# One step of a recurrent attention rebuilt: where the precomputed projections, the softmax waits and the output projection of the tail run

## The chip, the cores and the metric

The kernel runs on one core of one Trainium2 chip. The metric is the device time of one execution in microseconds. Three runs of the kernel before took 2381.08, 2387.85 and 2399.44 us, so the median is 2387.85 us. One execution was profiled; its own time is 2384.49 us and its span, from the first to the last instruction, 2382.6 us.

## The reference, cut to what matters

```python
# A: x [2048, 1024] in 64 segments of 32 rows; mem [8, 1024]; H = 32 heads of 128
mem = mem0
for s in range(64):
    h = concat([mem, x[32*s : 32*s+32]])          # 40 rows
    q, k, v = h @ Wq, h @ Wk, h @ Wv               # each 1024 -> 32 x 128
    p = softmax(mask(q @ k.T * 128**-0.5))         # per head, 40 x 40
    o = (p @ v) @ Wo                               # 4096 -> 1024
    mem = o[:8]                                    # goes into the next segment
    outs.append(o[8:])
a = concat(outs)
# B: a GEGLU feed-forward on x, 1024 -> 3584 -> 1024
b = (gelu(x @ w_gate) * (x @ w_up)) @ w_down
g = sigmoid(sum(x * gate_w))
return g * a + (1 - g) * b
```

The 64 segments are a chain: the memory rows of one are needed before the first projection of the next.

## The kernel before, in words

**Stages.** A first stage transposes x into scratch in DRAM and loads weights. Then come 64 steps, one for each segment, then a tail that multiplies the remaining attention rows by Wo, then the feed-forward.

**Rows.** A step projects 32 columns: the 24 first rows of its segment and the 8 memory rows (`hT`). The other 8 rows of each segment depend on no memory, so their q, k and v are computed for four segments at once, from the 32 columns in `hR`, by *fill units* (`fill`, L690): 8 pieces of 4 matmuls. A fill unit's result is copied out of PSUM, for q and k also transposed, put in one of the `stage` buffers and written to `qk_scr` or `v_scr` by DMAs that POOL issues; later steps read it back into `qkr` and `vB`. `FILL` (L738) says which of the six units of a group runs in which of four steps: two units, two, one and one. The attention output of these 8 rows is collected in `oRc`, written to `o_scr`, and multiplied by Wo in the tail (L867 to L886): 256 matmuls of 512 columns.

**Weights.** Wq, Wk, Wv and Wo are cut into 64 *pieces* of 512 KB ([128, 2048]). 53 slots of SBUF hold them. 42 pieces stay; 22 pieces form 11 pairs, the two of a pair sharing one slot (`PAIRS`, L304). Each step uses both halves r = 0 and r = 1 of every matrix and swaps their order from step to step (`at_step`), so each pair costs one fetch a step (`fetch`, `spent`): SP issues it as soon as the piece in the slot has been used, and it has to have landed when the other half of the same matrix comes to it.

**Order in a step.** `ORDER` (L310) gives 8 blocks of 8 pieces: k0 (positions p0 to p7), q0 (p8 to p15), v0 (p16 to p23), k1 (p24 to p31), q1 (p32 to p39), o0 (p40 to p47), v1 (p48 to p55), o1 (p56 to p63). A piece of k, q or v is 4 matmuls of 512 columns, on four column groups of the array at a time; a piece of o is 8 of 256 columns. `on(m, r, n, ...)` hooks other work in front of piece n of a block, in the program order of every engine: ACT copies a finished block to `tok` or `vA` (L570), PE transposes `tok` (L587), DVE copies that to `kT` or `qT` (L573), `scores` (L603) runs 33 small matmuls and the softmax on DVE and ACT into `tA` and `tB`, and `attend` (L634) multiplies those by `vA` and `vB` into four banks, from where ACT and DVE copy to `oT`, which the o block reads.

The first softmax is started before k1 and its attend stands in q1 at its sixth piece; the second is started before v1 and its attend stands before o1, with 6 pieces of a fill unit around v1 in the steps that have two units, 3 in the others. At the end of a step ACT copies the o result to `a_bf`, PE transposes it (L845) and DVE writes the 8 memory columns into `hT` (L848); other fill pieces stand around that transpose.

**Shared memory.** The tiles of the step share their bytes: `vA` lies on `oT`, and so does the stage buffer "o"; stage "k" lies on `kT` together with `pA` and `pB`; stage "q" on `qT` together with `tA`, `tB`, `E8` and `a_bf`. A tile is written only when every reader of the bytes is done, DMAs included: `vA` waits until the store of stage "o" has landed.

**Queues.** Each engine works in program order. SP issues the fetches. POOL issues the small DMAs of the step in one line with its own copies: after the end of a step it stores `a_bf`, then the fill results, then copies `qkr` into `kT` and `qT` (L732), then loads `qkr` and `vB`. These DMAs use a scratch of `RING` bytes in each partition (L253).

## Time and profile before

| | |
|---|---|
| median of three runs | 2387.85 us |
| profiled execution: its time, its span | 2384.49 us, 2382.6 us |
| PE busy | 2071.2 us, 87% of the span |
| DVE, ACT, POOL busy | 898.5 us (38%), 571.7 us (24%), 588.2 us (25%) |
| bytes moved by DMA | 542.61 MB, mean 228 GB/s |
| mean granted clock of TensorE | 0.984 |

The span falls into four stretches: up to 134.6 us the first stage and step 0; up to 1718.3 us the steps 1 to 63; up to 1778.8 us the tail with Wo; then the feed-forward, to the end. The three cuts are the end of step 0 and of step 63 (the copy to `a_bf`) and the first matmul of the feed-forward. Busy shares are averages over all of that; what matters for a change inside the step is what PE waits for inside a step. The time outside the span is 1.9 us.

### The profile page before, as it was taken

To read this page: it belongs to the slowest core of one execution; us is meant where nothing else is said; L and a number is where in the kernel's file an instruction comes from. 1 tells how busy PE (TensorE), PEld (TensorE's weight loads), DVE (VectorE), ACT (ScalarE), POOL (GpSimd) and SP (SyncE) were. 2 spreads that over 40 slices of the span, in tenths; PEclk is the share of its full clock that TensorE was granted. 3 is DMA by queue.
4 is the path that set the end of the run, shared out by engine and by line. 5 is a ranking of instruction groups with operands and counts; after the bars stand their busy time and mean duration, and the time that the engine had idled before them with its cause. 6 is when DMAs were issued, how large, how long until landed. Compare 5 with 4: busy or idle time off the path is not lost.

```text
span 2382.6 us, 76316 instructions
## 1 busy us (share of the span) xinstructions
PE 2071.2 (87%) x34822; PEld 1059.3 (44%) x34822; DVE 898.5 (38%) x2119; ACT 571.7 (24%) x1175; POOL 588.2 (25%) x1139
## 2 busy tenths in 40 slices
PE   2588888888888888898888988887799999999998
PEld 1244444444444444444444444444464444444443
DVE  3233333333333433334333333333215345263462
ACT  1122222222222222222222222222113123031230
POOL 5233323333233333333333333332200000000000
PEclk9899999999999999999999999998999999999999
DMA  9967776777767767778687776776872440804406
GB/s 355 371 224 243 267 262 235 267 260 265 269 227 253 280 221 285 255 245 290 229 289 246 256 262 239 274 263 212 278 245 109 155 146 1 291 9 145 156 1 229
DMA packets 207970, 542.61 MB, mean 228 GB/s; under 512 B 27288, under 2 KB 40472, under 8 KB 207648
## 3 DMA queue, kind: packets, MB, share of 16 engines
q1 hardware_dynamic: 174240, 483.99, 57.1%
...
q14 instruction: 49, 0.40, 0.0%
...
## 4 chain that ended last, share of the span: by engine, by line
PE 48%; DMA 25%; DVE 12%; issue 6%; ACT 5%; POOL 3%; ACTq 0%; SPq 0%; POOLq 0%
PE pb L918 14%; PE pb L683 10%; PE pb L955 6%; DMA vB<-v_scr 6%; DMA v_scr<-oS 5%; DMA qk_scr<-oS 5%; PE pb L671 5%; PE pb L698 4%; DMA sl<-in_A_Wq_dram 3%; PE pb L877 2%; DMA a_scr<-a_bf 2%; DMA wd<-in_B_w_down_dram 2%; DVE st L620 2%; PE pb L587 2%; POOL v_scr L709 2%
## 5 line engine op out<-in xcount | busy, mean ns | idle before, releaser
L671 PE MATMUL pb<-sl,hT 128*32 128x512 bf16 x12288 | 780.5, 384 | 52.5 <-DMA sl<-in_A_Wk_dram 21.3
L671 PEld LDWEIGHTS pb<-sl,hT 128*32 128x32 bf16 x12288 | 316.6, 96 | 350.8 <-DMA sl<-in_A_Wk_dram 38.6
L683 PE MATMUL pb<-sl,oT 128*32 128x256 bf16 x8192 | 277.4, 282 | 2.6 <-ACT oT L570 2.1
L570 ACT ACTIVATE tok<-pb 128x512 bf16<-128x512 f32 x320 | 191.3, 598 | 319.0 <-PE pb L671 265.3
L683 PEld LDWEIGHTS pb<-sl,oT 128*32 128x32 bf16 x8192 | 211.1, 100 | 60.4 <-ACT oT L570 24.8
L698 PE MATMUL pb<-sl,hR 128*32 128x512 bf16 x3072 | 226.5, 391 | 7.1 <-issue 6.0
L918 PE MATMUL pb<-xT,wg 128*128 128x512 bf16 x896 | 211.8, 379 | 8.4 <-DVE GT L934 8.4
L655 POOL COPY oRc<-oT 128x128 bf16<-128x128 bf16 x128 | 97.2, 759 | 466.5 <-DVE oT L573 466.5
L918 PE MATMUL pb<-xT,wu 128*128 128x512 bf16 x896 | 211.7, 379 | 0.0
L955 PE MATMUL pb<-wd,GT 128*128 128x512 bf16 x896 | 195.9, 379 | 3.4 <-DMA wd<-in_B_w_down_dram 3.3
L641 PE MATMUL pb<-tA,vA 32*128 32x40 bf16 x2048 | 36.5, 178 | 138.4 <-DVE tB L631 94.5
L570 ACT ACTIVATE vA<-pb 128x512 bf16<-128x512 f32 x128 | 76.4, 597 | 289.8 <-DMA v_scr<-oS 126.5
L926 ACT ACTIVATE s<-pb 128x512 f32<-128x512 f32 x112 | 66.8, 596 | 319.8 <-PE pb L918 300.3
L918 PEld LDWEIGHTS pb<-xT,wg 128*128 128x128 bf16 x896 | 86.9, 98 | 116.3 <-DVE GT L934 12.8
L573 DVE COPY kT<-pb 128x512 bf16<-128x512 bf16 x128 | 54.3, 424 | 217.8 <-POOL kT L732 121.2
L955 PEld LDWEIGHTS pb<-wd,GT 128*128 128x128 bf16 x896 | 86.7, 98 | 111.9 <-DMA wd<-in_B_w_down_dram 9.5
L918 PEld LDWEIGHTS pb<-xT,wu 128*128 128x128 bf16 x896 | 87.7, 98 | 105.7
L616 DVE TENSOR_REDUCE st<-pb 128x8 f32<-128x320 f32 x128 | 62.9, 491 | 169.3 <-PE pb L611 169.3
L573 DVE COPY qT<-pb 128x512 bf16<-128x512 bf16 x128 | 54.3, 424 | 192.0 <-PE pb L587 182.5
L927 DVE SCALAR_TENSOR_TENSOR tp<-s,pb 128x512 f32<-128x512 f32 x112 | 76.9, 686 | 131.7 <-ACT s L926 131.6
L570 ACT ACTIVATE oT<-pb 128x160 bf16<-128x160 f32 x256 | 63.8, 301 | 215.0 <-PE pb L646 215.0
L641 PEld LDWEIGHTS pb<-tA,vA 32*128 32x128 bf16 x2048 | 25.0, 92 | 199.0 <-DVE tB L631 97.3
...
## 6 DMA issues: line engine op xcount, KB each, us to landing
sl<-in_A_Wv_dram SPq DMA_DIRECT2D x268, 512.0 KB, 10.4
sl<-in_A_Wk_dram SPq DMA_DIRECT2D x205, 512.0 KB, 6.0
sl<-in_A_Wq_dram SPq DMA_DIRECT2D x142, 512.0 KB, 9.1
sl<-in_A_Wo_dram SPq DMA_DIRECT2D x142, 512.0 KB, 6.0
wd<-in_B_w_down_dram SPq DMA_DIRECT2D x56, 1024.0 KB, 6.5
qkr<-qk_scr POOLq DMA_DIRECT2D x128, 64.0 KB, 5.8
...
```

The lines of the kernel that those rows point to most:

```text
L570: op("act", lambda e: e.activation(o, i, ACTF.Copy), rd=rd, wr=wr)
L573: op("dve", lambda e: e.tensor_copy(o, i), rd=rd, wr=wr)
L616: op("dve", lambda e: e.tensor_reduce(nm, sS, AX.X, ALU.max, negate=True), rd=[BK(SS)], wr=[st8.r(0, 8)])
L641: e.matmul(PB[bo[g]][:, j * LQ:(j + 1) * LQ], lhsT=vA[r, j, :], rhs=tA[r, 2 * j:2 * j + 2, :].rearrange("p a c -> p (a c)")[:, 0:LQ], star ...
L655: op("pool", lambda e: e.tensor_copy(oRc[:, :, 16 * u:16 * u + 16].rearrange("p c x -> p x c"), oT[:, :, :, 32:40].rearrange("p g j c -> p ...
L671: ins = e.matmul(PB[bk][32 * g:32 * g + 32, :], lhsT=h[:, i, :], rhs=w[:, g * 512:(g + 1) * 512], start=(p % 8 == 0), stop=(p % 8 == 7))
L683: ins = e.matmul(PB[XO][32 * g:32 * g + 32, 0:256], lhsT=oT[:, gp_, 2 * jj + hh, 0:32], rhs=w[:, c:c + 256], start=(r == 0 and p % 8 == 0 ...
L698: ins = e.matmul(PB[b][32 * g:32 * g + 32, :], lhsT=h[:, k[2], :], rhs=w[:, g * 512:(g + 1) * 512], start=(n == 0), stop=(n == 7))
L918: ins = e.matmul(PB[bk][:, 0:FB], lhsT=w[:, kc, cc:cc + 128], rhs=xT[:, :, :, kc, :].rearrange("p t i c -> p (t i) c"), start=(kc == 0), s ...
L926: op("act", lambda e, hg=hg: e.activation(s1[:, :], hg, ACTF.Square, scale=SQ), rd=[BK(bg)], wr=[s1.r()])
L927: op("dve", lambda e, hg=hg, t=t: e.scalar_tensor_tensor(out=t[:, :], in0=s1[:, :], scalar=1.0, in1=hg, op0=ALU.add, op1=ALU.mult), rd=[BK ...
L955: ins = e.matmul(PB[bank[2 * k + hf]][:, :], lhsT=GT[:, j, tb * 128:(tb + 1) * 128], rhs=w[:, jj, hf * 512:(hf + 1) * 512], start=(j == 0) ...
```

## The change

**The fill units and where they run.** Every step now has up to two units, one in front of o0 (`f1`, bank F1) and one in front of o1 (`f2`, bank F2). The first attend stands inside f1 (4 pieces, attend, 1 piece, the transpose of q1, 3 pieces), the second inside f2 (5 pieces, attend, 3 pieces). f2 is a q or v unit in each of four steps. f1 is a k unit in two of four steps; in the other two it is a *Wo unit* (`wo`): 8 pieces with the shape of the o pieces, that multiply the collected rows of four earlier segments by one half of Wo. Their two halves are added (`part`, `add_part`) and stored by POOL (`store_tail`). The tail stage is gone but for the last four segments: `last_tail` runs after seven of the 28 blocks of the feed-forward's first part, and the loads w3, w4 and of w_down come behind it.

**The end of a step.** No fill pieces stand around the memory transpose any more. The copy to `a_bf`, the transpose and the copy into the next `hT` are cut in halves, for the even and the odd pieces of k; k0 uses the even pieces first. There are two `hT`, so the next segment's load is issued during q1.

**Buffers.** The two stage buffers, `pA` and `pB` have bytes of their own; `a_bf` lies on `pA`. `qkr` exists twice, and the scores read the q part from it, so that one POOL copy (`rest_k`) remains of two; it stands before the end of the step.

**Weights.** 12 pairs in 52 slots, so 12 fetches a step: k 2 (were 3), q 2, v 5 (were 4), o 3 (were 2). **Ring.** `RING` goes from 4096 to 2048 bytes. The rest of the memory freed holds `oR`, `part` and `oR2`.

**Step 0** computes one fill unit more (q0 of group 1), and its three units for r = 1 stand in front of the first scores instead of behind the first attend.

The diff, cut; lines that the region of the step loses are those of the functions printed above.

```diff
-        RING = 4096
+        RING = 2048
...
-        hT = al("hT", [128, KC, 32])
+        hTs = [al(f"hT{n}", [128, KC, 32]) for n in range(2)]
         hR = al("hR", [128, KC, 32])
         low = cur[0] = (cur[0] + 63) // 64 * 64
-        qkr = al("qkr", [128, 2, 128])
-        oRc = al("oRc", [128, NB, 32])
+        qkr = al("qkr", [128, 2, 2, 128])
+        oRc = al("oRc", [128, 2, NB, 16])
         vB = al("vB", [128, 2, 128])
         kT = al("kT", [128, 4, 4, LQ])
-        qT = al("qT", [128, 4, 4, LQ])
+        qT = al("qT", [128, 4, 4, 32])
         oT = al("oT", [128, 4, 4, LQ])
         tok = al("tok", [128, 512])
+        stage = [al(f"stg{n}", [128, 512]) for n in range(2)]
+        pA = al("pA", [128, 8, 32])
+        pB = al("pB", [128, 288])
+        a_bf = al("a_bf", [128, 256], at=pA.off)
         vA = al("vA", [128, 4, 128], at=oT.off)
-        pA = al("pA", [128, 8, 32], at=kT.off)
-        pB = al("pB", [128, 288], at=kT.off + 512)
-        E8 = al("E8", [128, 8, LQ], at=qT.off + 640)
         tA = al("tA", [128, 8, 32], at=qT.off)
         tB = al("tB", [128, 8, 32], at=qT.off + 512)
-        a_bf = al("a_bf", [128, 256], at=qT.off)
-        stage = {n: al(n + "S", [128, 512], at=t.off) for n, t in (("k", kT), ("q", qT), ("o", oT))}
+        E8 = al("E8", [128, 8, LQ], at=qT.off + 384)
 
         PIECE = 4096
         cur[0] = (cur[0] + 63) // 64 * 64
         res0 = cur[0]
         NLOW = (hole - RING) // PIECE
+        odd0 = RING + NLOW * PIECE
+        assert hole - odd0 >= 2048
+        oR = al("oR", [128, RB, 16], at=odd0)
+        part = al("part", [128, 256], FP32, at=odd0 + 1024)
+        oR2 = al("oR2", [128, RB, 16], at=odd0 + 1024)
         NSLOT = NLOW + (top - cur[0]) // PIECE
 
 
-        PAIRS = {"k": (1, 3, 5), "q": (0, 2), "v": (0, 2, 4, 6), "o": (0, 2)}
+        PAIRS = {"k": (0, 2), "q": (0, 2), "v": (0, 1, 2, 4, 6), "o": (0, 2, 4)}
 
         def seq(m, r):
             p = [i for i in range(8) if i in PAIRS[m]]
...
         def load_h(s):
-            op("pool", lambda e: e.dma_start(hT[:, :, :].rearrange("p k c -> p (k c)"), xq_scr[s // 4, :, s % 4, :]),
-               rd=[("D", "xq", s // 4)], wr=[hT.r()], lane="h")
+            t = hTs[s % 2]
+            op("pool", lambda e: e.dma_start(t[:, :, :].rearrange("p k c -> p (k c)"), xq_scr[s // 4, :, s % 4, :]),
+               rd=[("D", "xq", s // 4)], wr=[t.r()], lane=f"h{s % 2}")
 
...
+        def scores(r, mid=None):
...
-                            ins = e.matmul(PB[SS][32 * g:32 * g + hi - lo, j * 80 + c:j * 80 + c + LQ], lhsT=qT[:, j, g, lo:hi],
-                                           rhs=kT[:, j, g, :], start=False, stop=True, skip_group_check=True)
+                            x = 8 * (4 * j + g)
+                            ins = e.matmul(PB[SS][32 * g:32 * g + hi - lo, j * 80 + c:j * 80 + c + LQ],
+                                           lhsT=qT[:, j, g, :] if lo == 0 else qkr[:, r, 0, x:x + 8], rhs=kT[:, j, g, :], start=False, stop=True, skip_group_check=True)
                 return ins
-            op("pe", f, rd=[qT.r(), kT.r(), ident.r(), mS.r()], wr=[BK(SS)])
...
+        bank_of = {("k", 0): B0, ("q", 0): B1, ("v", 0): B2, ("k", 1): B0, ("q", 1): F2, ("v", 1): B0}
...
-                op("pe", f, rd=[h.r(), w.r()], wr=[BK(bk)])
+                op("pe", f, rd=[h.r(32 * i, 32 * i + 32), w.r()], wr=[BK(bk)])
...
+        def wo(u, b, t=oR, ends=(True, True), at_end=False):
+            out = []
+            for i in range(8):
+                w = (xo.get(("o", u, i)) if at_end else None) or slots[home["o", u, i]]
+
+                def f(e, i=i, w=w):
+                    for hh in range(2):
+                        for g in range(4):
+                            c = hh * 1024 + g * 256
+                            ins = e.matmul(PB[b][32 * g:32 * g + 32, 0:256], lhsT=t[:, :, 2 * i + hh], rhs=w[:, c:c + 256],
+                                           start=(ends[0] and i == 0 and hh == 0), stop=(ends[1] and i == 7 and hh == 1))
+                    return ins
+                out.append(lambda f=f, w=w: op("pe", f, rd=[t.r(), w.r()], wr=[BK(b)]))
+            return out
+
+        def store_tail(Q, t):
+            for g in range(4):
+                op("pool", lambda e, g=g: e.dma_start(a_scr[4 * Q:4 * Q + 4, NR:SEG, 256 * g:256 * g + 256],
+                                                      t[32 * g:32 * g + 32, 0:256]),
+                   rd=[t.r(0, 256)] + [("D", "a", x) for x in range(4 * Q, 4 * Q + 4)], wr=[("D", "ar", Q, g)], lane=f"ar{g}")
...
+        def rest_k(r):
+            op("pool", lambda e: e.tensor_copy(kT[:, :, :, 32:40].rearrange("p j g c -> p (j g) c"),
+                                               qkr[:, r, 1, :].rearrange("p (x c) -> p x c", c=8)),
+               rd=[qkr.r(256 * r + 128, 256 * r + 256)], wr=[kT.r()])
...
-        FILL = ((("k", 1), ("q", 1)), (("q", 0), ("v", 0)), (("v", 1),), (("k", 0),))
-        X, Y = A0, A1
+        FILL1 = {3: ("k", 0), 0: ("k", 1)}
+        FILL2 = {3: ("q", 0), 0: ("q", 1), 1: ("v", 0), 2: ("v", 1)}
         for s in range(NSEG):
             last = s == NSEG - 1
             at = {}
             ua, ub = s % 2, 1 - s % 2
+            h_next = hTs[1 - s % 2]
             G = (s + 1) // 4 + 1
-            fl = [(m, u, G) for m, u in FILL[s % 4]] if G < NG else []
-            bank_of.update({mr: (X, Y)[n % 2] for n, mr in enumerate(KQV)})
-            bko = dict(bank_of)
-            fill_bank = (X, Y)
-            f1 = fill(*fl[0][:2], X) if fl else []
-            f2 = fill(*fl[1][:2], Y) if len(fl) > 1 else []
+            Q = s // 4 - 1
+            k1 = FILL1.get(s % 4) if G < NG else None
+            k2 = FILL2[s % 4] if G < NG else None
+            uw = {1: 1, 2: 0}.get(s % 4) if Q >= 0 else None
+            f1 = fill(*k1, F1) if k1 else wo(uw, F1) if uw is not None else []
+            f2 = fill(*k2, F2) if k2 else []
 
             def on(m, r, n, *fs):
                 at.setdefault(base_of[m, r] + n, []).extend(fs)
                     f()
                 del fs[:n]
 
...
+            on("k", 0, 4, some(pend))
...
+            on("k", 1, 0, lambda: scores(0))
+            on("k", 1, 3, lambda: rest_k(1))
+            on("q", 1, 0, lambda: evac(bank_of["k", 1], tok))
+            if not last:
+                on("q", 1, 0, lambda: load_h(s + 1))
+                on("q", 1, 1, lambda: load_qk(s + 1, 0))
+                on("v", 1, 2, lambda: load_qk(s + 1, 1))
+            on("q", 1, 4, lambda: trans(kT))
+            if s % 4 == 0 and Q >= 0:
+                on("q", 1, 2, lambda: load_oR(Q, 1))
+            if s % 4 == 1 and Q >= 0:
+                on("o", 0, 3, lambda: load_oR(Q, 0))
+            def add_part():
+                op("dve", lambda e: e.tensor_tensor(out=stage[0][:, 0:256], in0=PB[F1][:, 0:256], in1=part[:, :], op=ALU.add),
+                   rd=[BK(F1), part.r()], wr=[stage[0].r(0, 256)])
+            on("o", 0, 0, lambda: evac(bank_of["q", 1], tok))
+            on("o", 0, 0, some(f1, 4))
+            on("o", 0, 0, lambda: attend(ua))
+            on("o", 0, 0, some(f1, 1))
+            on("o", 0, 0, lambda: trans(qT))
+            on("o", 0, 0, some(f1))
+            if k1:
+                on("o", 0, 1, lambda: fill_evac(*k1, F1, stage[0]))
+            if uw == 1:
+                on("o", 0, 1, lambda: act_copy(part[:, :], PB[F1][:, 0:256], [BK(F1)], [part.r()]))
+            on("o", 0, 1, lambda: scores(1, add_part if uw == 0 else None))
+            if k1:
+                on("o", 0, 6, fill_trans)
+                on("o", 0, 6, lambda: fill_put(stage[0], "act"))
+                on("o", 0, 6, lambda: fill_store(*k1, G, stage[0]))
+            if uw == 0:
+                on("o", 0, 6, lambda: store_tail(Q, stage[0]))
+            on("o", 1, 0, lambda: evac(bank_of["v", 1], vA))
+            if not last:
+                on("o", 1, 0, lambda: rest_k(0))
+            on("o", 1, 0, some(f2, 5))
             on("o", 1, 0, lambda: attend(ub))
+            on("o", 1, 0, some(f2))
+            if k2:
+                on("o", 1, 1, lambda: fill_evac(*k2, F2, stage[1]))
             def o_store(s=s):
+                op("pool", lambda e: e.dma_start(o_scr[s].rearrange("p u c -> p (u c)"), oRc[:, :, :, :].rearrange("p u c x -> p (u c x)")),
+                   rd=[oRc.r()], wr=[("D", "o", s)], lane="sto")
+            on("o", 1, 2, o_store)
             if last:
                 for n, f in enumerate(early):
                     on("o", 1, 1 + n, f)
             for p in range(64):
                 run(at.get(p, []))
                 proj(p, s)
+            for t in range(2):
+                cs = slice(128 * t, 128 * t + 128)
+                act_copy(a_bf[:, cs], PB[XO][:, cs], [BK(XO)], [a_bf.r(cs.start, cs.stop)])
+            if k2 and k2[0] == "q":
+                fill_trans()
             if not last:
+                for t, bk in enumerate((B1, B2)):
+                    op("pe", lambda e, t=t, bk=bk: e.transpose(PBV[bk][:, 0:128], a_bf[:, 128 * t:128 * t + 128], ident[:, :]),
+                       rd=[a_bf.r(128 * t, 128 * t + 128), ident.r()], wr=[BK(bk)])
+                    op("dve", lambda e, t=t, bk=bk: e.tensor_copy(
+                        h_next[:, :, NR:32].rearrange("p (g t) c -> p t g c", t=2)[:, t],
+                        PBV[bk][:, 0:128].rearrange("p (g c) -> p g c", g=4)[:, :, NR:32]),
+                       rd=[BK(bk)], wr=[h_next.r(32 * kc, 32 * kc + 32) for kc in range(t, KC, 2)])
+            if k2 and k2[0] == "q":
+                fill_put(stage[1], "dve")
+            def store(s=s, k2=k2, G=G):
                 op("pool", lambda e: e.dma_start(a_scr[s].rearrange("r (g c) -> g r c", g=4), a_bf[:, :]), rd=[a_bf.r()],
                    wr=[("D", "a", s)], lane="st")
+                if k2:
+                    fill_store(*k2, G, stage[1])
             pend.append(store)
             f()
+        load_oR(NG - 1, 1, oR2)
+        load_oR(NG - 1, 0)
+        def last_tail():
+            for f in wo(1, XO, oR2, (True, False), True) + wo(0, XO, oR, (False, True), True):
+                f()
+            t = oR2
+            a_last = al("a_last", [128, 256], at=t.off)
+            act_copy(a_last[:, :], PB[XO][:, 0:256], [BK(XO)], [a_last.r()])
+            store_tail(NG - 1, a_last)
+            load_w(3)
+            load_w(4)
+            for n in range(3):
+                load_wd()
         C_GELU = 0.7978845608028654
         SQ = 0.044715 ** 0.5
...
             for j in range(NJ):
+                if fb == 0 and j == sum(CH[:2]):
+                    last_tail()
```

## Rows read from the trace of the kernel before

**Rows 1.** Stretches of the span: start:end, length, busy by engine, clock, DMA share, GB/s.

```profile
134.60:1718.30 1583.70, 1368.38 (x31020) 728.40 (x31012) 581.45 (x1633) 409.93 (x907) 533.94 (x1073) 0.98 0.73 257
1718.30:1778.80 60.50, 56.73 (x256) 36.93 (x257) 2.07 (x3) 2.77 (x5) 0.73 (x1) 0.97 0.76 245
```

**Rows 2.** PE's groups in the steps: busy, mean ns, then idle and its releasers.

```profile
L671 PE MATMUL pb<-sl,hT 128*32 128x512 bf16 x12096 | 765.2, 382 | 52.5 <-DMA sl<-in_A_Wk_dram 21.3 <-ACT vA L570 18.7 <-issue 4.5
...
L641 PE MATMUL pb<-tA,vA 32*128 32x40 bf16 x2016 | 35.9, 178 | 133.9 <-DVE tB L631 94.5 <-DMA vB<-v_scr 38.9
```

**Rows 3.** ACT's groups in the steps: the copy of v out of PSUM.

```profile
L570 ACT ACTIVATE vA<-pb 128x512 bf16<-128x512 f32 x126 | 75.2, 597 | 279.6 <-DMA v_scr<-oS 120.2 <-DMA qk_scr<-oS 96.7 <-PE pb L671 62.7
```

**Rows 4.** PE in order of time, one step: start, length, operation, idle before.

```profile
1064.53 0.29 PE L845 MATMUL pb<-ident,a_bf 128*128 128x128 bf16 x2
1064.75 1.05 PE L698 MATMUL pb<-sl,hR 128*32 128x512 bf16 x16
1065.62 2.98 PE L671 MATMUL pb<-sl,hT 128*32 128x512 bf16 x52
...
1074.65 1.75 PE L671 MATMUL pb<-sl,hT 128*32 128x512 bf16 x24 [0.69 <-DMA sl<-in_A_Wk_dram]
1077.49 0.27 PE L641 MATMUL pb<-tA,vA 32*128 32x40 bf16 x16 [1.10 <-DVE tB L631]
...
1082.47 0.31 PE L611 MATMUL pb<-kT,qT 128*32 128x40 bf16 x21 [0.85 <-issue]
...
1084.33 0.82 PE L698 MATMUL pb<-sl,hR 128*32 128x512 bf16 x12
1086.53 0.28 PE L641 MATMUL pb<-tA,vA 32*128 32x40 bf16 x16 [1.38 <-DVE tB L631]
...
1086.77 0.61 PE L698 MATMUL pb<-sl,hR 128*32 128x512 bf16 x8
1087.27 1.93 PE L683 MATMUL pb<-sl,oT 128*32 128x256 bf16 x64
1089.02 0.60 PE L698 MATMUL pb<-sl,hR 128*32 128x512 bf16 x8
1089.69 0.29 PE L845 MATMUL pb<-ident,a_bf 128*128 128x128 bf16 x2
```

**Rows 5.** All engines in order of time: one softmax from scores to tB.

```profile
1030.30 0.31 PE L606 MATMUL pb<-mS,ident 128*128 128x320 bf16 x1
...
1034.15 0.40 DVE L631 STREAM_TRANSPOSE tB<-pB 128x256 bf16<-128x256 bf16 x1
```

**Rows 6.** PE in order of time: the end of a step without fill units.

```profile
1667.46 0.29 PE L845 MATMUL pb<-ident,a_bf 128*128 128x128 bf16 x2 [0.48 <-ACT a_bf L570]
1668.03 2.99 PE L671 MATMUL pb<-sl,hT 128*32 128x512 bf16 x52 [0.28 <-DVE hT L848]
```

**Rows 7.** One step's fetches (line L360): issues, first and last start; time to landing.

```profile
L360 SPq DMA_DIRECT2D sl<-in_A_Wv_dram x4: 328/468/803, 1017.6 to 1019.4; - x4
L360 SPq DMA_DIRECT2D sl<-in_A_Wk_dram x3: 328/341/435, 1013.1 to 1014.1; - x3
...
DMA to landing us min/median/max: 4.1/8.0/11.3
```

**Rows 8.** A stretch in which fetches alone run: columns as in Rows 1.

```profile
1023.00:1028.00 5.00, 3.90 (x72) 1.78 (x68) 2.91 (x9) 1.46 (x5) 1.33 (x3) 0.73 1.04 406
```

**Rows 9.** DMA issues by line: count, KB each, median us to landing.

```profile
xT<-xq_scr SPq DMA_DIRECT2D x4, 1024.0 KB, 6.3
...
vB<-v_scr POOLq DMA_DIRECT2D x63, 64.0 KB, 6.3
v_scr<-oS POOLq DMA_DIRECT2D x124, 32.0 KB, 5.6
...
wg<-in_B_w_gate_dram SPq DMA_DIRECT2D x1, 512.0 KB, 8.7
```

**Rows 10.** POOL in order of time, the start of a step.

```profile
1091.24 2.18 POOL L709 DMA_DIRECT2D v_scr<-oS  x4 [0.59 <-ACT oS L570]
```

More of the change, by code (lines that the diff above doesn't have):

```diff
@@ L514, in al2 @@
             raise AssertionError(name)
-        asb = [al2(f"asb{t}", [128, D]) for t in range(4)]
         tp = [al2(f"tp{t}", [128, FB], FP32) for t in range(2)]
         s1 = al2("s1", [128, FB], FP32)
+        assert s1.off < res0
+        asb = [al2(f"asb{t}", [128, D]) for t in range(4)]
         dsb = [al2(f"dsb{t}", [128, 512], FP32) for t in range(2)]
@@ L812, in bass_gated_mix__memory_aug_recurrent_mem_tr__geglu_ffn__prompt_kernel @@
-            on("q", 1, 6, lambda: trans(kT, "dve"))
-            on("q", 1, 7, rest_1)
-            on("o", 0, 0, lambda: evac(bko["q", 1], tok, "act"))
-            on("o", 0, 4, lambda: trans(qT, "dve"))
-            on("v", 1, 0, lambda: scores())
-            two = len(fl) > 1
-            n1, n2, n3 = (3, 3, 8) if two else (0, 3, 2)
-            on("v", 1, 0, some(f1, n1))
-            on("o", 1, 0, lambda: load_h(s + 1) if not last else None)
-            on("o", 1, 0, lambda: evac(bko["v", 1], vA, "act"))
@@ L852, in bass_gated_mix__memory_aug_recurrent_mem_tr__geglu_ffn__prompt_kernel @@
-            run(fb)
-            def store(s=s, fl=fl[-1:], b=Y if two else X):
+            for t in range(2):
+                cs = slice(128 * t, 128 * t + 128)
+                act_copy(a_bf[:, cs], PB[XO][:, cs], [BK(XO)], [a_bf.r(cs.start, cs.stop)])
+            if k2 and k2[0] == "q":
+                fill_trans()
+            if not last:
+                for t, bk in enumerate((B1, B2)):
[5 more added lines that the diff above has]
+                       rd=[BK(bk)], wr=[h_next.r(32 * kc, 32 * kc + 32) for kc in range(t, KC, 2)])
```

230 lines of the change are left out of this document (72 added, 158 removed).

## The prediction, made before the changed kernel was run

> **What bounds the kernel now.** I read the busy time by stretches first. The steps 1 to 63 take 1583.7 of 2382.6 us and the tail 60.5 us [rows 1]; the other two stretches are hardly touched. Two attends in each of 63 steps make the 2016 matmuls of L641 (32 a step), so a step lasts 1583.7 / 63 = 25.14 us. Second, PE's groups in that stretch: before the attends and the projections PE stands idle for 133.9 + 52.5 = 186 us [rows 2], 3.0 us a step, mostly for tB, the end of a softmax. Third, why tB is late: ACT's copy to vA waits 120.2 + 96.7 us for stores of the stage buffer "o" to land [rows 3]; the exponential of the first softmax stands behind that copy on ACT. Fourth, one step in order of time [rows 4]: 25.16 us from memory transpose to memory transpose, with four gaps of 0.69, 1.10, 0.85 and 1.38 us. So the step is bound by PE's work plus waits that shared buffers and too little cover cause. Fifth, the fetches: DMA is busy 0.73 of the stretch [rows 1], and this is the resource that the change loads more.
>
> **PE's own time in the new step.** In rows 4 the four gaps sum to 4.0 us. Each also costs a drained pipeline, about 0.18 us (the o block is 1.93 us long, the next operation starts after 1.75), together 0.7. 25.16 - 4.0 - 0.7 = 20.4 us is work, with 44 / 4 = 11 fill pieces in it.
> - The new step has 16 such pieces, Wo pieces included. A piece costs 0.87 / 4 = 0.22 us (1064.75 to 1065.62); a Wo piece has the shape of an o piece, 1.75 / 8 = 0.22 us. Five more: +1.1.
> - The end of a step loses its cover. Without fills, o's end to the next projection takes 0.48 + 0.29 + 0.28 = 1.05 us [rows 6], with the drain 1.2; halving the copies should take off 0.2. So 1.0 us in place of the 0.22 us that the transposes cost inside the fills (1064.53 to 1064.75): +0.8.
> - Transposes of k fills in front of o0's seventh piece: four, at 0.11 us each by the same rows, in two of four steps: +0.2. Those of q fills run while ACT copies to a_bf: nothing.
> - For pauses of the kind "issue" (0.85 in this step) I allow 0.3.
>
> Sum: 20.4 + 1.1 + 0.8 + 0.2 + 0.3 = **22.8 us**.
>
> **Where the stalls go.** A softmax takes 4.25 us from the first score matmul to the end of tB [rows 5]. Between scores and attend now lie 16 pieces of k1 and q1 and 4 of f1, then 7 of o0, 8 of v1 and 5 of f2: 20 x 0.22 = 4.4 us each, before the scores' own time is counted. So both are covered, narrowly, in full steps. Steps 3 to 58 are full, 56 of them. Without units the cover is 16 and 15 pieces, 3.5 and 3.3 us, so about 2 us of waiting come back where 3.5 us of pieces are saved: 21.5 us. The wait of vA goes, since no stage lies on oT. On POOL the copies into kT and qT no longer stand behind the stores; the load of vB still does. After the store of a_bf and at most four stores (2.18 us [rows 10]) it is issued some 3.5 us into the step and lands 6.3 us later [rows 9], at 10, before the first attend at 11 to 12. The load of the next hT has its own buffer and moves to q1, so POOL no longer waits for PE there.
>
> **What is late next: the fetches.** In one step [rows 7] the nine fetches of k, q and v, from 1013.1 to the last landing 1019.4 + 11.3 = 1030.7, take 17.6 us, 1.96 us a piece with the wait for the first data and the small DMAs among them. A piece of 0.524 MB in a stretch of fetches alone takes 0.524 MB / 406 GB/s = 1.29 us [rows 8]. The new step again has nine fetches before o (2, 2 and 5), then three instead of two. From p0 on: first issue 0.3, ninth landing 17.9, needed at p55, which PE reaches at 22.8 - 1.0 - 4.0 = 17.8 (behind it one piece, f2, an attend and o1: 0.22 + 1.76 + 0.24 + 1.75). The three o pieces are issued around 14, so they queue behind: 17.9 + 3 x 1.29 = 21.8, and I add 0.6 for the small DMAs that used to run after the burst: 22.4. The last is needed at p63, at 21.6. So PE waits 0.8 us there, and the step is 22.4 + 0.22 + 1.0 = **23.6 us**. The ends: 22.8 if the stream hides; 25.0 if all twelve keep the pace of the nine (0.3 + 12 x 1.96 + 1.2). I take 23.6, since the last pieces run behind the burst, where rows 8 were taken. Steps with fewer units lack the 0.6: 23.0.
>
> Here a rule has to be weighed. Rows 8 show 406 GB/s over 5 us into this one core. The Trainium skill, DMA: Bandwidth & Descriptors, section "Where 436 GB/s comes from", has the HBM side bind at about 358 GB/s for one core. By that rule, as an estimate, a piece takes 1.46 us, twelve take 2.0 us more, the step 25.6 and the kernel some 2370; this trace speaks against it with its 406.
>
> **Tail.** 60.5 us [rows 1] go, with the 256 matmuls. In their place: the feed-forward's first loads had that time as cover and now have not. Behind p55 of step 63 SP issues three pieces (3.9 us), xT (6.3 to landing) and w0 (8.7) [rows 9]: one after another 18.9, fully overlapped some 11 (3.1 MB at 406 GB/s and a latency of 3 to 4). PE ends its step about 3 us behind p55, so it waits 8 to 16 us; I take 11. The last Wo units cost 16 x 0.22 = 3.5 us plus a wait for bank 0, which the feed-forward's seventh block still reads: between nothing and the unit's own length, I take 2. A slower clock after the wait and a late w1: 2. Together 18.5, so -42. w3, w4 and the w_down loads move behind the last Wo unit on SP, with seven blocks of 16 matmuls (at 0.22 us 25 us) before w3 is needed: nothing. Step 0 has one unit more (1.8 us) and three moved ahead into its wait for scratch: I take zero, +-5.
>
> **Sum.** 56 x 23.6 + 7 x 23.0 = 1482.6, plus 5 for stretches at the lower clock (the stretch's mean is 0.98 now): 1487.6 in place of 1583.7, -96. 2384.5 (the profiled execution, 3.4 us under the median of 2387.85) - 96 - 42 = 2246; I say **2245**.
>
> **Rivals.**
> - **The stream hides** and PE alone sets the step: 56 x 22.8 + 7 x 21.5 + 5 = 1432, -151: **2190**. For it: DMA idles 0.27 of the time now, and part of the 17.6 us is waiting of SP for slots. Against it: the two loops differ by 0.8 us.
> - **The burst's pace holds for all twelve**, since the shorter step packs the same small DMAs more densely: 63 x 25.0 + 5 = 1580, -4, and the tail: **2340**. The waits for tB become waits for Wv and Wo. The 358 GB/s case belongs here.
> - **Slower: the halved ring holds back POOL's DMAs.** POOL issues about 11 a step (a_bf, three fill stores on average, vB, hT, two qkr, o, half an oR, one tail store, hR at times), each 5.6 to 6.3 us to landing [rows 9]. If only two can be in flight, they take 11 x 5.6 / 2 = 31 us, with 2 to 3 us of copies 33; the step follows, since vB and qkr come through this queue: 63 x 33 = 2079, +495, with the tail **2840**. With three in flight it is 23, and hides; below three it decides. Now four stores are issued within 2.18 us [rows 10] while each takes 5.6, so at least four are in flight at twice the ring. No row shows how many the ring holds. The Trainium skill, Perfetto Trace Analysis, section "DMA Instruction — SWDGE (GPSIMD)", has the DMA engine begin before the instruction is through when more descriptors are made than fit the buffer, which would lengthen POOL's issues; no issue in these rows is that long.
>
> **How the numbers follow.** The forecast (2215 to 2285, the waits at p55 and p63 between 0.3 and 1.5 us) 0.55; hidden stream 0.24; burst's pace 0.12; ring 0.05; waits not named here 0.04. Range 2175 to 2320: it reaches over most of the hidden stream (2190 less step 0's 5 and some) and half way to the burst's pace. About 1% is what a measurement of this kernel can tell from no change; faster by more: 0.55 + 0.24 + 0.10 + 0.03, same 0.03, slower 0.05.
>
> **What would show it.** PE's idle in front of L641 falls from 133.9 to under 30 us; vA no longer waits for stores; a new wait of L683 and L671 for fetches of Wo and Wv of 30 to 60 us in all; about 0.9 us between o and the next k0; DMA share up from 0.73 to over 0.8; the feed-forward begins about 11 us after step 63. I am wrong if attends still wait for tB (the cover of 4.4 against 4.25 us is thin), if POOL's issues grow beyond 0.8 us, or if k1 waits for its pieces.

## The result and the profile after

The changed kernel takes 2309.55 us (median of four runs, 2306.34 to 2315.05) against 2384.69 beside it: a ratio of 0.968, 95% interval 0.963 to 0.972. It is faster by 75 us where 140 were forecast. The profiled execution has a span of 2304.5 us against 2382.6.

By stretches, with the columns of [rows 1]: steps 1 to 63, the time from the last step to the first feed-forward matmul, and the feed-forward with the last Wo units in it:

```profile
140.10:1681.10 1541.00, 1408.18 (x32871) 800.68 (x32868) 586.64 (x1682) 442.45 (x1012) 556.15 (x1033) 0.99 0.80 288
1681.10:1688.70 7.60, 0.00 (x0) 0.02 (x1) 0.00 (x0) 0.32 (x2) 1.51 (x2) 0.75 1.08 375
1688.70:2304.50 615.80, 588.51 (x2796) 264.71 (x2816) 273.25 (x400) 138.40 (x226) 3.14 (x5) 0.99 0.39 137
```

Step 0 ends 5.5 us later (140.1 for 134.6). The steps take 42.7 us less, the end 40.9 less (7.6 + 615.8 for 60.5 and the 603.8 from 1778.8 to the end). Together -78.1, the difference of the spans. The forecast had 0, -96 and -42: what is missing is missing in the steps.

PE's groups in the steps, which answer to [rows 2]: busy, mean ns of one, then the idle time in front and what ended it.

```profile
L670 PE MATMUL pb<-sl,hT 128*32 128x512 bf16 x12096 | 744.2, 382 | 43.2 <-DMA sl<-in_A_Wq_dram 18.4 <-issue 8.5 <-DMA sl<-in_A_Wv_dram 7.9
L682 PE MATMUL pb<-sl,oT 128*32 128x256 bf16 x8064 | 277.4, 275 | 56.2 <-issue 46.1 <-DMA sl<-in_A_Wo_dram 7.6 <-ACT oT L576 2.1
...
L641 PE MATMUL pb<-tA,vA 32*128 32x40 bf16 x2016 | 35.6, 178 | 7.2 <-issue 3.7 <-ACT vA L576 3.5
```

The attends no longer wait for a softmax: 133.9 became 7.2 us. The copy to vA, in ACT's groups, waits for PE alone, for no store [rows 3]:

```profile
L576 ACT ACTIVATE vA<-pb 128x512 bf16<-128x512 f32 x126 | 75.2, 597 | 264.2 <-PE pb L670 264.2
```

In exchange the o blocks (L682) stand idle for 56.2 us, 46.1 of it "issue": PE waits for nothing that the profile's events show. The same blocks in the kernel before:

```profile
L683 PE MATMUL pb<-sl,oT 128*32 128x256 bf16 x8064 | 273.2, 282 | 2.6 <-ACT oT L570 2.1 <-issue 0.2
```

Over all of PE's groups in the steps, "issue" is 65.6 us; it was 21.1.

One step of PE in order of time, as in [rows 4]:

```profile
1043.00 0.40 PE L871 MATMUL pb<-ident,a_bf 128*128 128x128 bf16 x2 [0.38 <-ACT a_bf L576]
1043.49 2.99 PE L670 MATMUL pb<-sl,hT 128*32 128x512 bf16 x52
...
1054.48 0.40 PE L670 MATMUL pb<-sl,hT 128*32 128x512 bf16 x4 [0.38 <-DMA sl<-in_A_Wq_dram]
1054.71 1.05 PE L712 MATMUL pb<-sl,oR 128*32 128x256 bf16 x32
1055.69 0.37 PE L641 MATMUL pb<-tA,vA 32*128 32x40 bf16 x16
...
1058.22 1.40 PE L682 MATMUL pb<-sl,oT 128*32 128x256 bf16 x44
1061.62 0.51 PE L682 MATMUL pb<-sl,oT 128*32 128x256 bf16 x12 [2.00 <-issue]
1061.94 1.91 PE L670 MATMUL pb<-sl,hT 128*32 128x512 bf16 x32
...
1064.87 0.27 PE L641 MATMUL pb<-tA,vA 32*128 32x40 bf16 x16
...
1068.10 0.40 PE L871 MATMUL pb<-ident,a_bf 128*128 128x128 bf16 x2 [0.39 <-ACT a_bf L576]
```

Both attends start without a gap; of the 25.1 us, 2.0 are one pause inside an o block, after 52 of its 64 matmuls. Four short stretches of that step show what the DMA does then (the last two numbers: DMA share and GB/s):

```profile
1043.50:1045.00 1.50, 1.50 (x28) 0.76 (x32) 0.11 (x1) 0.00 (x0) 1.48 (x3) 1.00 0.07 11
1053.00:1059.00 6.00, 5.62 (x182) 3.99 (x182) 2.80 (x8) 1.09 (x3) 1.03 (x2) 1.00 1.03 414
1059.60:1061.60 2.00, 0.02 (x3) 0.00 (x0) 1.71 (x6) 0.39 (x1) 1.44 (x3) 1.00 0.99 370
1066.00:1067.70 1.70, 1.70 (x64) 1.28 (x52) 0.00 (x0) 0.59 (x1) 1.20 (x2) 1.00 0.01 5
```

The DMA is full in the middle of a step, the pause included, and empty at its ends. One entry in the page's list of queues bears on the pause: instructions come over the same DMA engines, in 287 packets of 4.70 MB / 287 = 16.4 KB. How these packets and the pauses hang together is worked out behind the experiments.

```profile
q8 instruction: 287, 4.70, 0.8%
```

### The profile page after: what moved, and what is told of

Read it like the earlier page. It is cut to its first block, busy times and chain, and to the rows that moved or that the text cites. A ratio compares the mean times of both kernels' runs of the same rounds, so it can differ in the third digit from the quotient of the medians.

```text
span 2304.5 us, 80168 instructions
## 1 busy us (share of the span) xinstructions
PE 2060.9 (89%) x36594; PEld 1099.2 (48%) x36614; DVE 901.2 (39%) x2164; ACT 604.1 (26%) x1280; POOL 616.0 (27%) x1107
## 4 chain that ended last, share of the span: by engine, by line
PE 65%; DMA 24%; issue 5%; DVE 3%; ACT 2%; POOL 1%; SPq 0%; ACTq 0%; POOLq 0%; DVEq 0%
PE pb L670 20%; PE pb L929 14%; DMA sl<-in_A_Wq_dram 11%; PE pb L682 9%; PE pb L697 6%; PE pb L966 6%; DMA sl<-in_A_Wo_dram 5%; PE pb L712 3%; PE pb L588 3%; DMA sl<-in_A_Wv_dram 3%; DMA wd<-in_B_w_down_dram 2%; PE pb L609 1%; DMA xr_scr<-xr 1%; PE pb L641 1%; PE pb L603 1%
## 5 line engine op out<-in xcount | busy, mean ns | idle before, releaser
L670 PE MATMUL pb<-sl,hT 128*32 128x512 bf16 x12288 | 756.8, 383 | 43.2 <-DMA sl<-in_A_Wq_dram 18.4
L670 PEld LDWEIGHTS pb<-sl,hT 128*32 128x32 bf16 x12288 | 331.7, 97 | 327.2 <-DMA sl<-in_A_Wq_dram 38.8
L682 PE MATMUL pb<-sl,oT 128*32 128x256 bf16 x8192 | 281.8, 275 | 56.2 <-issue 46.1
L682 PEld LDWEIGHTS pb<-sl,oT 128*32 128x32 bf16 x8192 | 213.0, 97 | 98.7 <-issue 54.6
L697 PE MATMUL pb<-sl,hR 128*32 128x512 bf16 x3072 | 215.0, 390 | 19.6 <-DMA sl<-in_A_Wq_dram 7.3
L579 DVE CAST oT<-pb 128x160 bf16<-128x160 f32 x256 | 71.2, 320 | 230.4 <-PE pb L646 230.4
L966 PEld LDWEIGHTS pb<-wd,GT 128*128 128x128 bf16 x896 | 86.4, 98 | 117.2 <-DMA wd<-in_B_w_down_dram 15.5
L588 PE MATMUL pb<-ident,tok 128*128 128x128 bf16 x1280 | 128.1, 222 | 13.2 <-ACT tok L576 8.9
L588 PEld LDWEIGHTS pb<-ident,tok 128*128 128x128 bf16 x1280 | 72.6, 98 | 123.2 <-ACT tok L576 94.3
L697 PEld LDWEIGHTS pb<-sl,hR 128*32 128x32 bf16 x3072 | 83.3, 98 | 81.5 <-DMA sl<-in_A_Wq_dram 8.4
```

Of the source, the lines that this page charges most:

```text
L579: op("dve", lambda e: e.tensor_copy(o, i), rd=rd, wr=wr)
L588: ins = e.transpose(PBV[TT][:, j * 128:(j + 1) * 128], tok[:, j * 128:(j + 1) * 128], ident[:, :])
L670: ins = e.matmul(PB[bk][32 * g:32 * g + 32, :], lhsT=h[:, i, :], rhs=w[:, g * 512:(g + 1) * 512], start=(p % 8 == 0), stop=(p % 8 == 7))
L682: ins = e.matmul(PB[XO][32 * g:32 * g + 32, 0:256], lhsT=oT[:, gp_, 2 * jj + hh, 0:32], rhs=w[:, c:c + 256], start=(r == 0 and p % 8 == 0 ...
L697: ins = e.matmul(PB[b][32 * g:32 * g + 32, :], lhsT=h[:, k[2], :], rhs=w[:, g * 512:(g + 1) * 512], start=(n == 0), stop=(n == 7))
L966: ins = e.matmul(PB[bank[2 * k + hf]][:, :], lhsT=GT[:, j, tb * 128:(tb + 1) * 128], rhs=w[:, jj, hf * 512:(hf + 1) * 512], start=(j == 0) ...
```

## The experiments

All times are medians of four runs; the ratio is to the kernel before, run beside it (2392 to 2398 us, by call), with its 95% interval. The changed kernel stands at 0.968. "Step" is the mean distance of the memory transposes of neighbouring steps (62 distances): 25.14 us before, 24.50 in the changed kernel.

**1. No fetches.** `spent` fetches nothing, so the weights of the first fetches are used throughout.

```diff
-            if done[n] < len(uses[n]) and uses[n][done[n]] != k:
-                fetch(n)
```

> The changed kernel without the 12 fetches of a step (the shared slots keep their first piece, so wrong weights are used; the matmuls are the same). It ran in 2309.6 us; PE's pauses of the kind issue before the o pieces (L682) sum to 46.1 us, its waits for pieces to some 40. Theory I, PE runs out of instructions where they are densest, whatever the DMA does: issue before o stays at 35 to 55, only the waits for pieces go, 2265 to 2280 us. Theory L, PE's instruction blocks are late because they share the DMA engines with the weights: issue before o under 10, 2205 to 2240 us.

Measured: 2146.08 us, 0.898 (0.894 to 0.902), step 22.19. Faster than either expectation; "issue" before o goes as theory L said. PE's groups:

```profile
L668 PE MATMUL pb<-sl,hT 128*32 128x512 bf16 x12096 | 723.2, 380 | 6.2
L680 PE MATMUL pb<-sl,oT 128*32 128x256 bf16 x8064 | 259.6, 273 | 2.1 <-ACT oT L574 2.1
```

All of "issue" is gone with the load, in PE's other groups too, though PE executes the same instructions. The stream costs PE 24.50 - 22.19 = 2.3 us a step.

**2. Half the bytes.** The same twelve fetches, each with half its columns.

```diff
+                op("sp", lambda e: e.dma_start(half(dst(t, k)), half(src(k))), wr=[t.r()], lane=lane)
```

> Every fetch of a pair in the steps brings half its columns, so twelve fetches with half the bytes (the outputs are not the reference's). Between no fetches (2146 us) and all (2310 us) lie 163 us. Theory P (what the stream costs PE goes with its bytes): half of it stays, 2220 to 2235. Theory K (there is a knee: below it the transfers land in time, and blocks of instructions too): most of it goes, 2150 to 2190, with less than 10 us called issue in front of o and less than 10 us of waits for weights.

Measured: 2161.17 us, 0.903 (0.900 to 0.905), step 22.33. Theory K: half the stream costs 15 us, the other half 148. Over all of PE's groups in the steps 4.5 us of "issue" are left.

```profile
L676 PE MATMUL pb<-sl,hT 128*32 128x512 bf16 x12120 | 725.5, 380 | 6.5 <-issue 0.2
L688 PE MATMUL pb<-sl,oT 128*32 128x256 bf16 x8128 | 263.0, 273 | 2.5 <-ACT oT L582 2.1 <-issue 0.3
```

**3 and 4. Eleven fetches.** Without the third Wo pair, and without the fifth Wv pair.

```diff
+            ... and (k[0], k[2]) != ("o", 4):      # 3
+            ... and (k[0], k[2]) != ("v", 6):      # 4
```

> The changed kernel without the fetch of the third o pair, 11 a step (wrong weights in one piece). If the weight stream sets the end of the step, as the prediction had it (0.8 us of waiting a step), a piece less takes that away: 2260 to 2285 us. If PE's pauses for instructions set it and the stream mostly hides: 2295 to 2306 us.

> The fifth Wv pair is not fetched, so eleven fetches a step again, but the three Wo pairs stay (the outputs are not the reference's). Theory Q (the end of the stream is what costs: the last Wo lands late, and its place decides): the fetches before o end 1.3 us earlier, the Wo pairs are issued at the same time after PE's o pieces and land up to 1.3 us earlier, if the queue was full: 2285 to 2305. Theory L (a twelfth of the load is worth the same wherever it is taken): 2262 to 2275, as without the third Wo pair (2267).

Measured: 2267.38 us, 0.949 (0.943 to 0.954), step 23.93; and 2287.62 us, 0.956 (0.952 to 0.960), step 24.18. The first loses the waits for Wo (7.6 to nothing) and a quarter of the pauses in front of o (34.6 us left), and its time is the one expected if the stream sets the end of the step. The second was to tell a place in the step (Q) from the load alone (L) and its time lies in Q's range, but not for Q's reason: the waits for Wo grow to 10.0, and what falls is the wait of the projections. PE's groups of that run:

```profile
L670 PE MATMUL pb<-sl,hT 128*32 128x512 bf16 x12088 | 739.6, 382 | 24.0 <-DMA sl<-in_A_Wq_dram 13.5 <-issue 2.6 <-DMA sl<-in_A_Wv_dram 0.6
L682 PE MATMUL pb<-sl,oT 128*32 128x256 bf16 x8064 | 280.6, 276 | 56.6 <-issue 44.1 <-DMA sl<-in_A_Wo_dram 10.0 <-ACT oT L576 2.1
```

A twelfth of the bytes is worth 22 to 42 us out of 163, more than its share of 14, and where it is taken matters.

**5. The kernel before without fetches.** The edit of 1 in the kernel before.

> The kernel before, with no pair fetched in the steps (the first step's weights are used all through; the outputs are not the reference's), to set beside the changed kernel without fetches (2146 us). Theory A (the stream cost the old step little, since its waits for the softmax covered it): only the 52.5 us in front of the projections go in part, and the step falls from 25.1 to 24.3 to 24.8 us: 2325 to 2370. The rebuild alone, without the stream, is then worth 180 to 220 us, of which the stream takes back more than half. Rival B (the stream cost the old step as much as the new one, 2.3 us): step 22.8, 2235 to 2260, and the rebuild without the stream is worth only about 100 us.

Measured: 2266.47 us, 0.948 (0.946 to 0.949), step 23.32.

```profile
L669 PE MATMUL pb<-sl,hT 128*32 128x512 bf16 x12096 | 742.2, 381 | 1.1 <-DVE hT L846 1.1
...
L639 PE MATMUL pb<-tA,vA 32*128 32x40 bf16 x2016 | 35.4, 178 | 124.5 <-DVE tB L629 124.3
```

Neither theory's range holds it, B is nearer. The stream, with eleven fetches, cost the old step 1.8 us, and costs the new one 2.3. So the rebuild is worth 2266 - 2146 = 120 us without the stream, and 75 with it.

**6. Wo units 512 columns wide** (half as many matmuls; even and odd heads then give two sums, which are not added). The loop of the edit:

```diff
...
-                        for g in range(4):
-                            c = hh * 1024 + g * 256
+                        for g in (2 * hh, 2 * hh + 1):
+                            c = g * 512
...
```

> The Wo units of the steps with 4 matmuls of 512 columns a piece in place of 8 of 256 (same columns streamed, half the instructions; the sums are incomplete). Theory I: issue before the o pieces falls from 46 to 25 to 35, the steps with a Wo unit (24.8 and 24.6 us) come down to the others (24.35, 24.15), 2285 to 2300 us. Theory L: nothing changes, 2304 to 2315 us.

Measured: 2277.87 us, 0.953 (0.948 to 0.959), step 24.06: faster than either expectation. The pauses in front of o fall only from 46.1 to 40.1 us, "issue" in all from 65.6 to 51.3, and the waits for weights from 35 to 25. So not all of the 32 us are pauses, and what moved the weights' waits is not shown.

**7. The o blocks 512 columns wide**, the same edit there, with the sums not added either.

> The o blocks with 4 matmuls of 512 columns a piece in place of 8 of 256 (same columns, half the instructions; the sums are incomplete). Theory I: issue before the o pieces falls from 46 to under 15, 2260 to 2280 us. Theory L: it stays over 35, 2300 to 2312 us.

Measured: 2263.79 us, 0.946 (0.941 to 0.951), step 23.90, 255 packets of instructions instead of 287: theory I's time and theory I's idle. The line covers 62 of the 63 steps; the last adds nothing to either wait.

```profile
L682 PE MATMUL pb<-sl,oT 128*32 128x512 bf16 x3968 | 267.5, 385 | 30.5 <-DMA sl<-in_A_Wo_dram 20.5 <-issue 7.9 <-ACT oT L576 1.7
```

The pauses fall from 46.1 to 7.9 us, but waits for Wo grow from 7.6 to 20.5: PE now reaches the last o pieces before their weights. This is the wait that the forecast had named; the pauses had covered a part of it.

**8. vA shares a buffer again**, with the second stage.

```diff
-        vA = al("vA", [128, 4, 128], at=oT.off)
+        vA = al("vA", [128, 4, 128], at=stage[1].off)
```

> One buffer is shared again: vA lies on the second fill stage, as in the kernel before, instead of on oT; all else is the changed kernel. Theory A (the own buffers matter by themselves): a fill's store takes 5.6 us to land, the copy into vA is wanted about 6.7 us into the step and may start at 8 to 9, so the first softmax ends 1 to 2 us later; of that some 1 us shows in front of the attends: 2330 to 2370 us, idle before the attends up from 7 to 50 us or more, vA waiting for POOL's store again. Rival B (the 16 pieces in front of the scores and the units around the attends have room enough): 2300 to 2318, idle before the attends under 20 us.

Measured: 2306.10 us, 0.964 (0.962 to 0.966): no loss, rival B. ACT waits for stores as it used to, and the attends are hardly later for it:

```profile
L576 ACT ACTIVATE vA<-pb 128x512 bf16<-128x512 f32 x126 | 75.3, 597 | 359.6 <-PE pb L670 185.8 <-DMA v_scr<-stg 98.9 <-DMA qk_scr<-stg 70.4
...
L641 PE MATMUL pb<-tA,vA 32*128 32x40 bf16 x2016 | 35.5, 178 | 6.4 <-ACT vA L576 3.5 <-issue 2.2 <-DVE tB L631 0.6
```

**9. No cover.** All pieces of both units behind the attend.

```diff
-            on("o", 0, 0, some(f1, 4))
             on("o", 0, 0, lambda: attend(ua))
...
-            on("o", 1, 0, some(f2, 5))
             on("o", 1, 0, lambda: attend(ub))
```

> The attends are no longer inside the fill units: all pieces of both units run behind the attend, the order of everything else stays. Theory A (the cover is worth what it hides on PE's path): 4 pieces ahead of the first attend and 5 ahead of the second go, 0.87 and 1.1 us, and the softmax of 4.25 us is then covered by 3.5 and 3.3 us of pieces: 1 to 2 us a step in 56 steps, 2365 to 2420 us, with 60 to 120 us idle before the attends. Rival B (the weight stream and the pauses called issue set the step, the waits only change place): 2300 to 2330, the idle before the attends rises and that before the projections and o falls by as much.

Measured: 2338.39 us, 0.979 (0.976 to 0.981), step 24.90: between the two theories. 36.7 us of idle come back in front of the attends, and 24 go from the projections and o:

```profile
L670 PE MATMUL pb<-sl,hT 128*32 128x512 bf16 x12096 | 737.8, 381 | 31.8 <-issue 9.3 <-DMA sl<-in_A_Wq_dram 9.1 <-DMA sl<-in_A_Wv_dram 6.3
L682 PE MATMUL pb<-sl,oT 128*32 128x256 bf16 x8064 | 274.0, 277 | 43.4 <-issue 41.2 <-ACT oT L576 2.1
...
L641 PE MATMUL pb<-tA,vA 32*128 32x40 bf16 x2016 | 35.0, 178 | 43.9 <-ACT vA L576 43.9
```

**10. Both wide, whole.** o blocks, Wo units and last tail with 512 columns; the two sums are added for the memory rows by a matmul with a selection matrix, elsewhere on POOL in the feed-forward, so a_bf is twice as wide and stored in two pieces.

```diff
+                        for g in (2 * hh, 2 * hh + 1):      # o blocks and Wo units
...
+                for hh in range(2):
+                    op("pool", lambda e, hh=hh: e.dma_start(a_scr[hh, s]..., a_bf[64 * hh:64 * hh + 64, :]), ...)
```

> A kernel that computes the whole reference: o blocks, Wo units and the last tail with matmuls of 512 columns, half as many instructions; even and odd heads give two partial sums, added for the memory rows by a matmul with a selection matrix and for the other rows on POOL in the feed-forward. Theory I (the pauses are late blocks of instructions, so fewer instructions in o and in the units help together): gain of the two alone, 32 + 46 us, less 0.2 us a step for the longer end of a step and some us for the larger loads of the feed-forward: 2235 to 2270, idle before o under 25 us. Theory L (only the weight stream's load counts, and both single runs gained since PE was shifted against it): no better than the better of the two alone, 2262 to 2285.

Measured: 2348.93 us, 0.982 (0.980 to 0.984), step 24.98. Both theories missed. Of "issue" 2.9 us are left in all of PE's groups, but all weights are waited for (62 of the 63 steps):

```profile
L679 PE MATMUL pb<-sl,hT 128*32 128x512 bf16 x11904 | 749.7, 386 | 74.2 <-DMA sl<-in_A_Wq_dram 38.3 <-DMA sl<-in_A_Wv_dram 27.2 <-DMA sl<-in_A_Wk_dram 4.4
L691 PE MATMUL pb<-sl,oT 128*32 128x512 bf16 x3968 | 268.2, 384 | 38.5 <-DMA sl<-in_A_Wo_dram 35.9 <-ACT oT L585 1.7
```

In one step PE waits 0.91 us for the last Wo, at 1064.98, while the DMA share is 0.22. PE waits 0.49 us more at the end of the step, and then comes a stretch in which the granted clock falls to 0.50, that is 1.2 in place of 2.4 GHz. The third number from the end of a line is the mean clock of its stretch:

```profile
1062.80:1064.90 2.10, 1.20 (x20) 0.30 (x12) 0.00 (x0) 0.15 (x1) 0.73 (x2) 1.00 0.22 84
1066.40:1070.00 3.60, 3.60 (x40) 1.53 (x44) 0.18 (x1) 0.39 (x1) 3.50 (x6) 0.56 0.51 140
```

Why every weight comes later here than in 7 is not settled: the end of the step and POOL's two stores differ, and they were not tried apart.

**11. Only the Wo units wide, whole.** As 6, with the two sums added by one matmul a tail and stored in two pieces.

```diff
+                op("pe", lambda e: e.matmul(PB[b][0:64, 0:512], lhsT=Sel[:, :], rhs=t[:, 0:512], start=True, stop=True), ...)
```

> A kernel that computes the whole reference: of the two wider forms only the Wo units have 512 columns (half as many instructions in them), the o blocks stay as in the changed kernel. The sums of even and odd heads are added by one matmul with a selection matrix a tail, 0.4 us every fourth step, and the tail is stored in two pieces instead of four. Theory I (fewer instructions for PE to fetch while the DMA is loaded; the price is at the end of a step only where o is widened): the gain of the Wo units alone, 32 us, less some 6 us: 2275 to 2295. Theory X (the gain of 32 us came from the part of the sum that was left out, or from the placing of the run): 2300 to 2315.

Measured: 2290.56 us, 0.957 (0.954 to 0.960), step 24.30. It lies in theory I's range and is ahead of both kernels, by 19 us of the changed one. The pauses in front of o fall from 46.1 to 36.8, "issue" in all from 65.6 to 53.9, and the waits for weights from 35 to 29:

```profile
L685 PE MATMUL pb<-sl,oT 128*32 128x256 bf16 x8084 | 280.6, 275 | 51.7 <-issue 36.8 <-DMA sl<-in_A_Wo_dram 11.3 <-ACT oT L579 2.2
```

**12. One pair moved,** from Wv to Wk, in kernel 11.

```diff
-        PAIRS = {"k": (0, 2), "q": (0, 2), "v": (0, 1, 2, 4, 6), "o": (0, 2, 4)}
+        PAIRS = {"k": (0, 2, 4), "q": (0, 2), "v": (0, 2, 4, 6), "o": (0, 2, 4)}
```

> The kernel with the 512-column Wo units (2291 us, the whole reference computed), with one of the twelve pairs moved: 3 Wk, 2 Wq, 4 Wv and 3 Wo instead of 2, 2, 5 and 3. The same bytes, but 0.5 MB of them are issued about 3 us earlier, in a stretch in which the DMA was little used, instead of at the end of the burst in front of o0. Theory B (how the bytes are bunched decides: PE is held while the burst of Wv and Wo keeps all engines full): a twelfth off the burst is worth up to what leaving out the fifth Wv was (22 us), 2266 to 2282, with less idle called issue in front of o than 36.8 us. Theory T (the total decides): 2284 to 2298. A third way: the third Wk is now wanted by k1 while Wq queues behind it, and waits of the projections for Wk and Wq eat the gain, 2290 to 2310.

Measured: 2365.45 us, 0.986 (0.981 to 0.991), step 25.47: the third way, and far beyond its range.

```profile
L673 PE MATMUL pb<-sl,hT 128*32 128x512 bf16 x12032 | 752.8, 381 | 110.5 <-DMA sl<-in_A_Wq_dram 54.7 <-DMA sl<-in_A_Wk_dram 45.0 <-issue 3.1
```

and one of these waits in the order of time:

```profile
1049.79 0.40 PE L673 MATMUL pb<-sl,hT 128*32 128x512 bf16 x4 [1.77 <-DMA sl<-in_A_Wq_dram]
```

The last Wq of that step was issued by 1040.9 and is there at 1049.8, 8.9 us later. The same bytes, issued earlier, cost 75 us more: run 11 waits nothing to speak of for Wk, here it is 45.0 us, and the Wq behind it grows from 10.8 to 54.7. Both are wanted sooner after their issue than the Wv that was given up. The pauses in front of o do fall, to 28.2, as theory B had it.

## Why the prediction was right in sign and range, and wrong in size

The sign and most of the mechanisms of the stalls held; 65 us were missing. The range held with some luck: the time lies outside the forecast's own 2215 to 2285, and inside 2175 to 2320 only because that was drawn half way to the burst's pace. By its waits, 65.6 us of "issue" and 18.4 for Wq, the result is nearest to "waits not named here", which had 0.04.

**The step that failed: "The ends: 22.8 if the stream hides; 25.0 if all twelve keep the pace of the nine", and between them "I take 23.6".** The forecast puts the mean of the 63 steps at 1487.6 / 63 = 23.6 us. Without the low-clock term and the 0.3 for "issue", PE's own time in it is (56 x 22.5 + 7 x 21.2) / 63 = 22.4, which leaves 1.2 us for all that the stream does. Measured: 22.2 without the stream, and 2.3 for it. PE's own time was right to 0.2 us; the stream's price was set at half of what it is. 1.1 us x 63 = 69 us is more than the whole error of the steps (53).

Its parts can be set beside each other, summed over the steps. For weights awaited at p55 and p63 the forecast has 56 x 0.8 + 7 x 1.5 = 55 us, and PE waits 35. For "issue" it has 0.3 x 63 = 19, and it is 65.6. The rest is PE's busy time, 1408 us against 1366 in run 1: 42 us for which the forecast has no term but the 5 for the clock. The working took 0.18 us for a drained pipeline off the old step at each gap, and put none on the new one; how much of the 42 that is was not separated.

The working fell short in three places. It put the four gaps of [rows 4] down to shared buffers and too little cover, but one of them (0.69) waits for Wk and one (0.85) is "issue", and both kinds come from the stream: without it (run 5) the old kernel has neither. It let PE meet the stream only at its end, at p55 and p63, and gave the fetches before no price, though the old trace has 21.3 us of waits for Wk [rows 2]. In the new step the second Wq is wanted some 8 us after its issue and lands after 7.4 (the median of all Wq), so it is late as soon as the queue is fuller: 18.4 us of waits for Wq, which the forecast did not have. And it allowed 0.3 us a step for "issue", which is what the old kernel has (21.1 us in 63 steps), as if a fuller DMA would not change it.

**What the pauses are.** They are PE's program coming late. The instruction queue carries it, 256 instructions to a packet: run 7 has 32 packets fewer for 8192 PE instructions fewer (4096 matmuls and as many weight loads). The kept trace has the start and length of every packet of that queue, and PE's instructions can be counted in it. In the steps of the changed kernel 66 pauses called "issue" are longer than 0.3 us, 63.7 us together. All 66 begin a whole multiple of 256 PE instructions from each other, to within one, so each stands where a block of the program ends. And all 66 end 1.2 to 1.6 us after such a packet was through, although a packet comes only every 6 us (257 in 1541). The 19 such pauses in the kernel before, 20.7 us, and the 23 of run 7 show the same two things.

The packets are late rather than slow. The median packet takes 1.01 us, and 1.03 in run 1. But it begins when PE is 121 instructions into the block in front of it, where that is 18 in run 1 and 53 in run 2; at 256 PE has nothing left to run. It is the load that delays them, since the three kernels run the same PE program and have 65.6, 0 and 4.5 us of "issue". Fewer instructions help where they were densest: an o block, 64 matmuls and 64 weight loads, takes 1.95 us, so 256 instructions last some 3.9 us there, and twice that at 512 columns. Run 7 has 21.9 us of "issue" left. Where a packet is held up before it begins is not shown.

**Why the gains do not add.** Pause and late weight cover each other: run 7 took 38 us of pauses off o and got 13 of waits for Wo back; run 9 brought 37 us to the attends and took 24 elsewhere. Run 2 shows a load at which there is almost nothing of either: a DMA share of 0.55 from 400 to 1400 us, for 0.81 with all bytes, has 4.5 us of pauses and none of waits for weights. Where between the two they set in was not tried.

**Point by point.**
- Softmax covered: right, 133.9 to 7.2 us. The thin cover of 4.4 against 4.25 us held, and run 9 prices it: 29 us.
- vA free of stores: right in the trace, but worth nothing by itself (run 8). What the waits of [rows 3] cost with the old cover was not tried apart.
- Waits for Wo and Wv "of 30 to 60 us in all": wrong, they are 7.9 + 7.6 = 15.5, and 18.4 for Wq come beside them. DMA share over 0.8: 0.80. About 0.9 us between o and the next k0: in the step above o1 ends at 1067.72, the next k0 starts at 1068.60. None of the three signs of being wrong came: no wait for tB, no group of POOL's issues over 0.8 us, 1.3 us of waits for Wk.
- Tail: -42 forecast, -40.9 measured, with its parts shifted. The wait for the first loads is 7.6, not 11; the last Wo units take 3.65 us behind a wait of 1.78 (3.5 and 2 forecast); the first block takes 3.33 us where the later ones take 1.9; waits for w_down grow from 3.3 to 7.7, where the forecast has nothing.

```profile
1688.71 3.33 PE L929 MATMUL pb<-xT,wg 128*128 128x512 bf16 x8 [7.79 <-DMA wg<-in_B_w_gate_dram]
...
1716.27 0.45 PE L712 MATMUL pb<-xo,oR 128*32 128x256 bf16 x8 [1.78 <-DVE GT L945]
...
1719.92 1.90 PE L929 MATMUL pb<-xT,wg 128*128 128x512 bf16 x8
```

The last of these in PE's groups of the feed-forward:

```profile
L966 PE MATMUL pb<-wd,GT 128*128 128x512 bf16 x876 | 194.7, 379 | 8.9 <-DMA wd<-in_B_w_down_dram 7.7
```

- Step 0: 5.5 us longer, just outside the +-5.
- The rivals. The hidden stream (2190) did not come; with half the bytes the kernel is under it, at 2161. The burst's pace (2340) is nearer to the result than the forecast, but its waits, for Wv and Wo, are the smaller part of what came. The halved ring shows nowhere: the two largest groups of POOL's issues take 0.55 and 0.56 us, as before, and PE has no wait for a transfer of POOL's.

```profile
L456 POOL DMA_DIRECT2D qkr<-qk_scr x124 | 68.5, 553 | 4.7 <-PE pb L682 4.0 <-issue 0.2
L738 POOL DMA_DIRECT2D v_scr<-stg x120 | 65.6, 558 | 0.0
```

- The case of 358 GB/s: six microseconds in the step above ran at 414 GB/s, so this bound does not hold here. The Trainium skill, Perfetto Trace Analysis, section "Roofline" under "Engine Utilization", has the same: with one core active 358 is a share and not a limit, and the 16 DMA engines end at about 435 GB/s. The trace agrees, with its 414.
